# Scaling the three widest tiles of P on ScalarE in batches 0 and 1 of a decay attention with two feed-forward layers

## Chip, cores and metric

The kernel runs on one core of a Trainium2 chip. The metric is the device time of one launch in microseconds (us); lower is better. Three runs of the kernel before took 909.36 to 911.1 us, with a median of 910.57.

## What is computed

Four batches of eight heads of causal attention with a decay that is added to the scores, over 576 positions of 64 values; its output, 2304 rows of 512, goes through a feed-forward layer with Mish (2048 wide) and then through one with a maximum of three products (768 wide).

```python
def _attn_ref(q, k, v, f):
    scores = scale * np.matmul(q, k.transpose(0, 1, 3, 2))
    cum = np.cumsum(np.log(np.clip(f, 0.0001, 1.0)), axis=-1)
    decay = cum[:, :, :, None] - cum[:, :, None, :]
    scores = np.where(causal, -1000000000.0, scores + decay)
    attn = np.exp(scores - np.max(scores, axis=-1, keepdims=True))
    attn = attn / (np.sum(attn, axis=-1, keepdims=True) + 1e-09)
    return np.matmul(attn, v)
def _moe_ref(x, w_in, w_out):
    h = x @ w_in
    return (h * np.tanh(softplus(h))) @ w_out
def _moe2_ref(x, w1, w2, w3, w_out):
    return np.maximum(np.maximum(x @ w1, x @ w2), x @ w3) @ w_out
```

## The kernel before

**Attention.** Two heads make a pair; a batch has four pairs, so there are 16 pairs, eight of them in batches 0 and 1. A pair is done in two units of `scores`. Unit g = 0 makes four tiles of P: for each head 128 query rows against 128 keys, and 128 against 256. Unit g = 1 makes five: for each head 128 rows against 384 keys and against 512, and one tile with the last 64 rows of both heads against all 576 (its name is `P_None`). The index of a tile within its unit is `ci`, so that in unit 1 the tiles 2, 3 and 4 are the two of 512 columns and the one of 576.

Each tile passes through these steps. TensorE makes the scores (`sc`, L336). VectorE adds the decay `cb` and finds the row's extreme `mn` (L390). ScalarE takes the exponential in place and sums each row into `sums` (L396). When a part of the unit's tiles is through, the helper `scale_rows` lets VectorE add 1e-9 to the sums (L357) and take the reciprocals `rr` (L358), and GpSimd multiplies each tile by its column of `rr` (L360). Unit 0 has two such parts, of tiles 0, 1 and 2, 3; in unit 1 they are tiles 0, 1 and tiles 2 to 4. TensorE then turns the scaled P in blocks of 128 x 128 (`pp`, L429), VectorE and ScalarE by turns copy the result out of PSUM (`TA` and `TB`, L433 and L435), and TensorE multiplies by v (`av`, L415). ScalarE rounds the result to a high part `xh` (L131) and VectorE keeps the rest as `xl` (L137).

Before a pair's scores, q and k are turned on TensorE (`tr`, L312) and copied by ScalarE as `kT` and `qT` (L314, L315, L317). Three PSUM banks are shared by these turned tiles and by `pp`. GpSimd masks the decay tiles `cb` (L295, L299), which come by DMA.

**Conversion of w_in.** Beside the attention the first layer's weights, which lie in 64-bit numbers, are fetched (`wr`, L146, 16 transfers) and converted: ScalarE takes the absolute value (Abs, L156), GpSimd clamps it (L160), VectorE shifts and joins the bits in three steps (L163, L166, L170), ScalarE rounds to the high part `wi` (L131) and GpSimd subtracts for the low part (L137).

**The first layer** (`h`, L181 to L183, three products each of high and low parts) is run by TensorE between the steps of the attention, as soon as the rows of a block and a piece of w_in are there. After the last `h`, the rest is nearly TensorE's alone: `y`, `g`, `q` and `o`.

**Order.** Every engine runs its instructions in the order in which they were put on its queue. That order isn't the order of the program text: a list scheduler with a model of times sets it, by priorities. `scale_rows` has a raised priority.

Of the kernel before, what the change touches and what calls it, by code (L numbers as in the profile page):

```python
# [13 lines left out]
AF = mybir.ActivationFunctionType  # L14
# [18 lines left out]
BLK = 256  # L33
BLK2 = 512
LEAD = 2

# [26 lines left out]
def tile_decay_attention__mish_ff__max3_ff(  # L65
# [16 lines left out]
    nc = tc.nc  # L82
# [8 lines left out]
    scale = 1.0 / float(D) ** 0.5  # L91
# [186 lines left out]
    def decay(J, h, qt):  # L278

        c2, c4 = J["cb"]  # L280
        if h is None:
            return c4.rearrange("p (a c) -> p a c", c=288)
        t = c2[:, h]
        if qt == 0:
            return t[:, 5:6, :]
        if qt == 1:
            return t[:, 0:7:6, :]
        if qt == 2:
            return t[:, 0:3, :].rearrange("p b c -> p (b c)")[:, None, :]
        return t[:, 0:6, :].rearrange("p (a b) c -> p a (b c)", a=2)[:, :, 0:256]  # L290
# [10 lines left out]
    def prep(J):  # L301

        b, hp, raw = J["b"], J["hp"], J["raw"]
        qq = as_.tile([128, 512], F32, name="qT", bufs=2)
        kk = as_.tile([128, S], F32, name="kT", bufs=2)
        last, v_ = q4[J["i"] % 2], vs[J["i"] % 3]
        rest = att_psum("tr")
        for i, dst in ((1, kk), (0, qq)):
            tr = att_psum("tr")
            with queued(last_av):  # L310
                for c in range(4):
                    nc.tensor.transpose(tr[:, c * 128:c * 128 + 128], raw[i][:, c * 128:c * 128 + 128], ident)  # L312
                last_tr[:] = [nc.tensor.transpose(rest[:, i * 64:i * 64 + 64], raw[i][U, 512:640], ident[U, U])]
            nc.scalar.activation(dst[:, 0:512], tr, AF.Copy)  # L314
        nc.scalar.activation(kk[:, 512:S], rest[:, 64:128], AF.Copy)  # L315
        for h, rows in enumerate((U, L)):
            nc.scalar.activation(last[rows, h * 64:h * 64 + 64], rest[rows, 0:64], AF.Copy)  # L317
        for h in range(2):
            nc.sync.dma_start(
                v_[:, h * 256:(h + 1) * 256].rearrange("p (t d) -> p t d", t=4),  # L320
                v[b, 2 * hp + h, 0:512, :].rearrange("(t p) d -> p t d", t=4),
            )
        nc.sync.dma_start(
            v_[L, 512:640].rearrange("p (h d) -> p h d", h=2),
            v[b, 2 * hp:2 * hp + 2, 512:S, :].rearrange("h p d -> p h d"),
        )
        J.update(q=qq, q4=last, k=kk, vs=v_)
        mask_decay(J)

    def score_mm(J, h, qt, dst, c0, w):  # L330
        if h is None:
            lhs, rows = J["q4"], slice(0, 128)
        else:
            rows = (U, L)[h]
            lhs = J["q"][rows, qt * 128:qt * 128 + 128]
        nc.tensor.matmul(dst, lhs, J["k"][rows, c0:c0 + w], start=True, stop=True, skip_group_check=True)  # L336

    def scores(J, g):


        P = {}
        u = count["unit"]
        count["unit"] += 1
        sm = sums[u % 4]
        mn = aw.tile([128, 6], F32, name="mn", bufs=4)
        rr = aw.tile([128, 5], F32, name="rr", bufs=4)
        tiles = [(h, qt) for qt in ((0, 1) if g == 0 else (2, 3)) for h in range(2)]
        if g == 1:
            tiles.append((None, 4))
        made = []  # L350
        col = 0

        def scale_rows(part):

            cs = slice(part[0], part[-1] + 1)
            with tc.high_priority(400):
                nc.vector.tensor_scalar(rr[:, cs], sm[:, cs], 1e-9, None, op0=ALU.add)  # L357
                nc.vector.reciprocal(rr[:, cs], rr[:, cs])  # L358
                for ci in part:
                    nc.gpsimd.tensor_scalar(made[ci], made[ci], rr[:, ci:ci + 1], 1.0, op0=ALU.mult, op1=ALU.mult)  # L360

        for ci, (h, qt) in enumerate(tiles):
            wd = (qt + 1) * 128 if qt < 4 else S
            Pt = aw.tile([128, wd], F32, name=f"P{qt}_{h}", bufs=LEAD)
            made.append(Pt)
            if h is None:
                P[4] = Pt
            else:
                P[h, qt] = Pt
            cb = decay(J, h, qt)  # L370
            if h is None:
                cb = [cb[:, n:n + 1] for n in range(2)]
            else:
                cb = [cb]
            s0 = 128 if qt == 1 else 0
            if not h and qt != 1:
                count["sc"] += 1
                pair = (aps if count["sc"] % 2 or not eps else eps[0]).tile([128, 2, 512], F32, name="sc", bufs=1)
                for n in range(2):
                    if h is None:  # L380
                        score_mm(J, h, qt, pair[:, n, :288], 288 * n, 288)
                    else:
                        score_mm(J, n, qt, pair[:, n, :wd], 0, wd)
                if qt == 0:
                    for n in range(2):
                        score_mm(J, n, 1, pair[:, n, 128:384], 0, 256)
            for pi, (c0, w) in enumerate([(0, wd)] if qt < 4 else [(0, 288), (288, 288)]):
                sc = pair[:, h or pi, s0:s0 + w]
                like = lambda t: t.rearrange("p (a c) -> p a c", a=cb[pi].shape[1])
                nc.vector.tensor_tensor_reduce(  # L390
                    out=like(Pt[:, c0:c0 + w]), in0=like(sc), in1=cb[pi],
                    scale=-scale, scalar=(3e38 if pi == 0 else mn[:, col - 1:col]),
                    op0=ALU.add, op1=ALU.min, accum_out=mn[:, col:col + 1],
                )
                col += 1
            nc.scalar.activation(  # L396
                Pt, Pt, AF.Exp, scale=-1.0, bias=mn[:, col - 1:col], accum_out=sm[:, ci:ci + 1],
            )
            if ci == 1:
                scale_rows([0, 1])  # L400
        scale_rows(list(range(2, len(tiles))))
        return P

# [48 lines left out]
    def attention():  # L452
# [9 lines left out]
        pend = []  # L462
        for n in range(len(units) + LEAD):
            if n == 6 + LEAD:
                eps.clear()
                early.close()
                eps_h.append(sa.enter_context(tc.tile_pool(name="hps", bufs=2, space=PSUM, reuse_waits="tile")))
            if n < len(units):
                ji, g = units[n]
                pend.append((J[ji], g, scores(J[ji], g)))  # L470
            if n >= LEAD:
                unit = pend.pop(0)
# [5 lines left out]
            if n < len(units) and g == (ji == 0) and ji + 1 < len(jobs):  # L478
                prep(J[ji + 1])
            if n >= LEAD:  # L480
                next(rest, None)
# [315 lines left out]
    for ft in range(NF2):  # L797
        g = [gps[ft % 2].tile([128, BLK2], F32, name=f"g{m}") for m in range(3)]
# [126 lines left out]
```

## Time and profile before

| | |
|---|---|
| median of 3 runs | 910.57 us (909.36 to 911.1) |
| the profiled execution | 909.78 us |
| its span, first to last instruction | 907.7 us |
| mean granted clock of TensorE | 0.992 of full speed |
| busy: TensorE, VectorE, ScalarE, GpSimd | 97%, 55%, 44%, 26% of the span |

The rows are read as follows. A group of instructions shows its line, engine, operation, output and inputs, shapes and count, then the busy time in us, the mean of one in ns, and the idle time just before with what ended it. A wait reads "engine line waited for engine line: us in total, times, the longest". PE is TensorE, PEld its weight loads, DVE VectorE, ACT ScalarE, POOL GpSimd, SP the queue that issues most DMAs.

### The profile page before, as it was taken

How to read it: one execution, taken by the hardware profiler on the slowest of the kernel's cores; microseconds unless marked ns; L12 is line 12 of the kernel's file. 1: busy time of each engine (PE TensorE's matmuls, PEld its weight loads, DVE VectorE, ACT ScalarE, POOL GpSimd, SP SyncE). 2: the span in 40 equal slices, each digit the busy share in tenths (PEclk: the TensorE clock that was granted, in tenths of full speed). 3: DMA queues.
4: the chain of work that ended last, by engine and by line, in shares of the span. 5: the costliest groups of instructions: out<-in, count | busy, mean ns of one | idle time of the engine just before them, and what ended most of it. 6: DMA issues, size and time to landing. Idle time of an engine off the chain costs nothing.

```text
span 907.7 us, 13930 instructions
## 1 busy us (share of the span) xinstructions
PE 882.8 (97%) x4800; PEld 704.8 (78%) x4800; DVE 497.1 (55%) x1186; ACT 400.7 (44%) x913; POOL 232.7 (26%) x317
## 2 busy tenths in 40 slices
PE   6898999999999999999999999999999999999998
PEld 3565666767767778889888888889888998889986
DVE  3598675344444343991367575775855447424440
ACT  4687666454443432533465545553433222412211
POOL 3689987222222220000020000000121332013310
PEclk8989999999999999999999999999999999999999
DMA  7896664444333115863456666663499444333401
GB/s 183 227 226 171 179 192 117 115 134 127 105 102 108 47 48 178 292 226 128 143 181 217 214 216 222 217 226 98 162 359 322 124 123 117 111 96 126 139 23 60
DMA packets 125030, 145.25 MB, mean 160 GB/s; under 512 B 64736, under 2 KB 78048, under 8 KB 124960
## 3 DMA queue, kind: packets, MB, share of 16 engines
q1 hardware_dynamic: 105856, 102.41, 39.0%
q10 hardware_dynamic: 16416, 27.79, 8.3%
q0 software_dynamic: 2688, 14.16, 4.3%
q8 instruction: 38, 0.62, 0.3%
q14 instruction: 32, 0.26, 0.1%
HBM read 102.83 MB, written 41.49 MB: 159 GB/s over the span
## 4 chain that ended last, share of the span: by engine, by line
PE 89%; POOL 3%; DMA 2%; DVE 2%; issue 1%; ACT 1%; SPq 1%; POOLq 0%
PE y L181 7%; PE y L183 7%; PE y L182 7%; PE h L181 7%; PE h L182 7%; PE h L183 7%; PE q L182 6%; PE q L183 6%; PE q L181 6%; PE sc L336 5%; PE av L415 5%; PE pp L429 5%; PE o L181 3%; PE o L182 3%; PE o L183 3%; PE g L181 2%
## 5 line engine op out<-in xcount | busy, mean ns | idle before, releaser
L181 PE MATMUL h<-xh,wi 128*128 128x512 f32 (+1 forms) x320 | 121.4, 380 | 1.6 <-ACT he L522 1.3
L182 PE MATMUL h<-xl,wi 128*128 128x512 f32 (+1 forms) x320 | 120.6, 377 | 1.8 <-DVE xl L137 1.8
L183 PE MATMUL h<-xh,wi 128*128 128x512 f32 (+1 forms) x320 | 120.7, 377 | 0.0
L182 PE MATMUL y<-gl,wo 128*128 128x512 f32 (+1 forms) x320 | 117.7, 368 | 0.0
L183 PE MATMUL y<-gh,wo 128*128 128x512 f32 (+1 forms) x320 | 117.6, 368 | 0.0
L181 PE MATMUL y<-gh,wo 128*128 128x512 f32 (+1 forms) x320 | 106.3, 368 | 0.0
L360 POOL TENSOR_SCALAR P<-P,rr 128x128 f32<-128x128 f32 (+3 forms) x128 | 74.0, 592 | 87.5 <-DVE rr L358 31.5
L659 DVE TENSOR_TENSOR gl<-g,gh 128x512 fp32r<-128x512 f32 x72 | 50.0, 697 | 83.3 <-ACT gh L658 83.1
L396 ACT ACTIVATE P<-P,mn 128x128 f32<-128x128 f32 (+3 forms) x128 | 70.7, 554 | 53.4 <-DVE mn L390 50.2
L652 ACT ACTIVATE g<-g 128x512 f32<-128x512 f32 x72 | 45.2, 632 | 70.6 <-DMA g<-h_d 65.7
L181 PEld LDWEIGHTS h<-xh,wi 128*128 128x128 f32 x320 | 60.1, 188 | 14.6 <-issue 2.2
L182 PEld LDWEIGHTS h<-xl,wi 128*128 128x128 f32 x320 | 60.1, 188 | 14.0 <-issue 2.8
L183 PEld LDWEIGHTS h<-xh,wi 128*128 128x128 f32 x320 | 60.3, 188 | 11.5 <-issue 2.7
L182 PEld LDWEIGHTS y<-gl,wo 128*128 128x128 f32 x320 | 60.3, 188 | 10.2
L183 PEld LDWEIGHTS y<-gh,wo 128*128 128x128 f32 x320 | 60.2, 188 | 10.1
L181 PEld LDWEIGHTS y<-gh,wo 128*128 128x128 f32 x320 | 60.3, 189 | 10.1
L522 ACT ACTIVATE he<-h 128x512 f32<-128x512 f32 x56 | 33.3, 595 | 57.0 <-PE h L183 52.4
L851 DVE TENSOR_TENSOR u<-q,p 128x448 f32<-128x448 f32 x36 | 22.4, 621 | 62.3 <-PE q L183 60.7
L336 PE MATMUL sc<-kT,qT 64*128 64x128 f32 (+3 forms) x256 | 51.9, 500 | 3.6 <-DVE mn L390 3.3
L429 PE MATMUL pp<-ident,P 128*128 128x128 f32 x320 | 51.1, 285 | 4.0 <-ACT qT L314 3.6
L658 ACT ACTIVATE gh<-g 128x512 fp32r<-128x512 f32 x72 | 45.0, 627 | 22.0 <-PE y L183 20.9
L429 PEld LDWEIGHTS pp<-ident,P 128*128 128x128 f32 x320 | 37.0, 143 | 20.1 <-issue 5.0
(141 smaller groups left out, 1850.3 us busy)
## 6 DMA issues: line engine op xcount, KB each, us to landing
g<-h_d SPq DMA_DIRECT2D x72, 256.0 KB, 2.9
s<-s_d SPq DMA_DIRECT2D x72, 256.0 KB, 3.0
h_d<-he ACTq DMA_DIRECT2D x56, 256.0 KB, 2.9
wr<-in_moe_w_out_dram SPq DMA_DIRECT2D x22, 512.0 KB, 4.6
wr<-in_moe_w_dram SPq DMA_DIRECT2D x24, 384.0 KB, 3.8
s_d<-sk POOLq DMA_DIRECT2D x12, 768.0 KB, 5.8
cb<-cum_d SPq DMA_DIRECT2D x32, 256.0 KB, 4.2
wr<-in_moe_w_in_dram SPq DMA_DIRECT2D x16, 512.0 KB, 4.5
```

What stands on the lines that cost most here:

```text
L181: nc.tensor.matmul(ps, wh, xh, start=start, stop=False, skip_group_check=True)
L182: nc.tensor.matmul(ps, wh, xl, start=False, stop=False, skip_group_check=True)
L183: return nc.tensor.matmul(ps, wl, xh, start=False, stop=stop, skip_group_check=True)
L336: nc.tensor.matmul(dst, lhs, J["k"][rows, c0:c0 + w], start=True, stop=True, skip_group_check=True)
L360: nc.gpsimd.tensor_scalar(made[ci], made[ci], rr[:, ci:ci + 1], 1.0, op0=ALU.mult, op1=ALU.mult)
L396: nc.scalar.activation(Pt, Pt, AF.Exp, scale=-1.0, bias=mn[:, col - 1:col], accum_out=sm[:, ci:ci + 1],)
L415: last = nc.tensor.matmul(acc[(U, L)[h], off:off + w], J["vs"][:, n * 64:n * 64 + 64], T[:, at[h]:at[h] + w], start=kt == 0 and off == 0, ...
L429: turn = nc.tensor.transpose(pp[:, n * 128:n * 128 + 128], Pt[:, k0:k0 + 128], ident)
L522: nc.scalar.activation(he, h, AF.Copy)
L652: nc.scalar.activation(g, g, AF.Mish)
L658: on_act[:] = [nc.scalar.activation(gh, g, AF.Copy)]
L659: on_dve[:] = [nc.vector.tensor_tensor(out=gl, in0=g, in1=gh, op=ALU.subtract)]
```

## The change

A table names, by unit, the tiles that ScalarE scales in batches 0 and 1. The others in these batches and all tiles of batches 2 and 3 stay with GpSimd. ScalarE's operation is a Copy with the reciprocals as a scale for each row.

```diff
+ON_ACT = {0: (), 1: (2, 3, 4)}
...
                 for ci in part:
+                    if J["b"] < 2 and ci in ON_ACT[g]:
+                        nc.scalar.activation(made[ci], made[ci], AF.Copy, scale=rr[:, ci:ci + 1])
+                        continue
                     nc.gpsimd.tensor_scalar(made[ci], made[ci], rr[:, ci:ci + 1], 1.0, op0=ALU.mult, op1=ALU.mult)
```

Since the scheduler sets the order anew, it differs on every engine from about the second pair until the first layer's end. In the changed kernel the lines up to L359 stand one further down and those from L360 on four (L156 is now L157, L360 is L364); the new operation is L362.

ScalarE around the first conversion, before (Abs is L156; the tiles 724, 730 and 737 belong to the third pair):

```order
L314 ACTIVATE kT<-tr 128x512
L396 ACTIVATE P_0_724,sums_172<-P_0_724,mn 128x384
L156 ACTIVATE wt<-wr 128x512
L396 ACTIVATE P_1_730,sums_172<-P_1_730,mn 128x384
L156 ACTIVATE wt<-wr 128x512
L314 ACTIVATE qT<-tr 128x512
L315 ACTIVATE kT<-tr 128x64
L317 ACTIVATE q_1_189<-tr 64x64 x2
L131 ACTIVATE xh_446<-av 128x256
L396 ACTIVATE P_0_737,sums_172<-P_0_737,mn 128x512
```

The same place now (Abs is L157; 518, 524 and the first P_None are the second pair's tiles):

```order
L362 ACTIVATE P_0_518<-P_0_518,rr 128x512
L362 ACTIVATE P_1_524<-P_1_524,rr 128x512
L362 ACTIVATE P_None<-P_None,rr 128x576
L400 ACTIVATE P_0_724,sums_172<-P_0_724,mn 128x384
L400 ACTIVATE P_1_730,sums_172<-P_1_730,mn 128x384
L157 ACTIVATE wt<-wr 128x512 x2
L315 ACTIVATE kT<-tr 128x512
L400 ACTIVATE P_0_737,sums_172<-P_0_737,mn 128x512
L316 ACTIVATE kT<-tr 128x64
L318 ACTIVATE q_1_189<-tr 64x64 x2
L400 ACTIVATE P_1_743,sums_172<-P_1_743,mn 128x512
L315 ACTIVATE qT<-tr 128x512
```

The second pair's three scalings stand ahead of the two Abs, as the first pair's do some rows further up. kT has moved from ahead of the Abs to behind both, and qT behind two exponentials of 512 columns.

GpSimd in the third pair, before:

```order
L160 TENSOR_SCALAR wt<-wt 128x512 x2
L360 TENSOR_SCALAR P_0_724<-P_0_724,rr 128x384
L360 TENSOR_SCALAR P_1_730<-P_1_730,rr 128x384
L137 TENSOR_TENSOR wi_148<-wt,wi_148 128x512
L295 AFFINE_SELECT cb<-cb 128x2x256
L295 AFFINE_SELECT cb<-cb 128x2x128 x2
L360 TENSOR_SCALAR P_0_737<-P_0_737,rr 128x512
L360 TENSOR_SCALAR P_1_743<-P_1_743,rr 128x512
L360 TENSOR_SCALAR P_None<-P_None,rr 128x576
L160 TENSOR_SCALAR wt<-wt 128x512
L299 TENSOR_TENSOR cb_819<-cb_819,mask_110 128x64
L360 TENSOR_SCALAR P_0_844<-P_0_844,rr 128x128
```

And now:

```order
L161 TENSOR_SCALAR wt<-wt 128x512
L364 TENSOR_SCALAR P_0_724<-P_0_724,rr 128x384
L364 TENSOR_SCALAR P_1_730<-P_1_730,rr 128x384
L161 TENSOR_SCALAR wt<-wt 128x512
L296 AFFINE_SELECT cb<-cb 128x2x256
L138 TENSOR_TENSOR wi_148<-wt,wi_148 128x512
L296 AFFINE_SELECT cb<-cb 128x2x128 x2
L300 TENSOR_TENSOR cb_819<-cb_819,mask_110 128x64
L364 TENSOR_SCALAR P_0_844<-P_0_844,rr 128x128
```

The three wide scalings are gone, and the next pair's first tile (844) follows the masks of cb at once.

## Rows read from the trace of the kernel before

**Rows 1.** The page's first part: busy time, share of the span, instructions.

```profile
PE 882.8 (97%) x4800; PEld 704.8 (78%) x4800; DVE 497.1 (55%) x1186; ACT 400.7 (44%) x913; POOL 232.7 (26%) x317
```

**Rows 2.** Stretches: length; PE, PEld, DVE, ACT, POOL busy (count); clock; DMA share, GB/s.

```profile
0.00:20.00 20.00, 11.36 (x38) 6.80 (x40) 6.41 (x29) 8.37 (x24) 4.99 (x20) 0.86 0.77 183
20.00:45.00 25.00, 21.36 (x143) 12.20 (x139) 15.19 (x66) 16.59 (x50) 16.75 (x32) 0.98 0.83 220
...
45.00:50.00 5.00, 4.62 (x22) 3.64 (x23) 4.63 (x14) 4.40 (x15) 3.52 (x4) 0.51 1.05 234
...
45.00:147.00 102.00, 94.22 (x631) 65.00 (x632) 82.02 (x225) 70.97 (x198) 94.50 (x99) 0.97 0.67 178
...
160.00:880.00 720.00, 719.60 (x3801) 593.34 (x3800) 387.69 (x845) 293.64 (x616) 110.84 (x156) 1.00 0.49 158
```

**Rows 3.** Waits of VectorE from 45 to 147 us.

```profile
DVE wt L163 <- POOL wt L160: 15.0, 10, 3.2
```

**Rows 4.** Groups of GpSimd's instructions from 45 to 147 us, forms kept apart.

```profile
L160 POOL TENSOR_SCALAR wt<-wt 128x512 f32<-128x512 f32 x16 | 30.8, 1927 | 3.7 <-ACT wt L156 2.9
...
L360 POOL TENSOR_SCALAR P<-P,rr 128x512 f32<-128x512 f32 x10 | 9.0, 907 | 0.3
...
L360 POOL TENSOR_SCALAR P_None<-P_None,rr 128x576 f32<-128x576 f32 x5 | 4.1, 829 | 0.0
```

**Rows 5.** Timeline of TensorE: start, length, operation, idle before and what ended it.

```profile
79.79 0.50 PE L182 MATMUL h<-xl,wi 128*128 128x512 f32 x1 [1.80 <-DVE xl L137]
...
85.13 0.92 PE L336 MATMUL sc<-kT,qT 64*128 64x384 f32 x4 [1.25 <-DVE mn L390]
...
106.83 0.88 PE L336 MATMUL sc<-kT,qT 64*128 64x384 f32 x2 [2.00 <-DVE mn L390]
...
145.97 0.50 PE L181 MATMUL h<-xh,wi 128*128 128x512 f32 x1 [1.32 <-ACT he L522]
```

**Rows 6.** The chain of work that ended last: start, length in us, what.

```profile
79.27 1.93 POOL wt L160
...
93.30 5.30 DMA cb<-cum_d
...
138.27 1.93 POOL wt L160
```

**Rows 7.** Groups of ScalarE's instructions, 45 to 147 us, and the last over the span.

```profile
L131 ACT ACTIVATE wi<-wt 128x512 fp32r<-128x512 f32 x16 | 10.0, 628 | 14.5 <-DVE wt L170 14.5
...
L396 ACT ACTIVATE P<-P,mn 128x512 f32<-128x512 f32 x12 | 8.6, 714 | 0.0
...
L396 ACT ACTIVATE P_None<-P_None,mn 128x576 f32<-128x576 f32 x16 | 12.4, 772 | 11.4 <-DVE mn L390 11.3
```

**Rows 8.** Busy time in the stretch from 25 to 35 us.

```profile
25.00:35.00 10.00, 9.89 (x67) 5.73 (x63) 8.66 (x41) 8.80 (x30) 8.04 (x16) 1.00 0.74 180
```

**Rows 9.** Timeline of SyncE's queue, ScalarE and TensorE: start, length, operation, idle before.

```profile
37.07 2.42 SPq L146 DMA_DIRECT2D wr<-in_moe_w_in_dram  x4
...
42.48 0.66 ACT L156 ACTIVATE wt<-wr 128x512 f32<-128x512 f32 x1 [3.85 <-DMA wr<-in_moe_w_in_dram]
...
44.75 0.58 ACT L314 ACTIVATE qT<-tr 128x512 f32<-128x512 f32 x1
...
45.38 1.11 PE L429 MATMUL pp<-ident,P 128*128 128x128 f32 x4 [3.61 <-ACT qT L314]
46.42 1.65 PE L336 MATMUL sc<-kT,qT 64*128 64x128 f32 x8
```

**Rows 10.** Timeline of GpSimd and of VectorE near 77 us.

```profile
77.21 1.26 POOL L137 TENSOR_TENSOR wi<-wt,wi 128x512 fp32r<-128x512 f32 x1
...
77.31 1.71 DVE L170 SCALAR_TENSOR_TENSOR wt<-wr,wt 128x512 int32<-128x512 int32 x1
```

**Rows 11.** One group of VectorE from 45 to 147 us, and from 160 to 350.

```profile
L357 DVE TENSOR_SCALAR rr<-sums 128x2 f32<-128x2 f32 x15 | 6.8, 450 | 0.5 <-ACT P L396 0.4
...
L357 DVE TENSOR_SCALAR rr<-sums 128x2 f32<-128x2 f32 x22 | 3.6, 166 | 7.9 <-ACT P L396 7.8
```

## The prediction

> **What bounds the kernel now.** The page's first part comes first: TensorE is busy 882.8 of 907.7 us [rows 1], so a change off TensorE can give back only its idle time, some 25 us. The table by stretches says where that lies [rows 2]: 8.6 us before 20 us, 3.6 from 20 to 45, 7.8 from 45 to 147, 0.4 from 160 to 880; what is left of the 25, some 4.5, lies nearly all after 880. The matmuls are the same before and after; a TensorE that never waits again after 147 us only begins earlier or later. So what the change is worth is settled before 147 us, and comes out at the end one for one.
>
> From 45 to 147 us GpSimd is busy 94.5 of 102 us, VectorE 82.0, ScalarE 71.0 [rows 2]. That is the stage in which w_in is converted beside attention. The waits agree: VectorE waits 15.0 us for GpSimd's clamp (L160), ten times, and ScalarE 14.5 us for the last step of the same conversion (L170) [rows 3, 7]. What GpSimd does there is 30.8 us of clamps, the low halves of w_in (L137), and scaling of P; the widest three tiles of five pairs are 9.0 + 4.1 = 13.1 us of it [rows 4].
>
> TensorE's timeline puts names to its idle time [rows 5]: 1.80 us before 80 us for xl, 1.25 before 85 and 2.00 before 107 for VectorE's score reduction, 1.32 before 146 for the copy of h. The chain of waits leads to the gap at 85 us from a clamp that began at 79.27, to the one at 146 from a clamp of 138.27, and to the one at 107 from a cb transfer of 5.30 us that began at 93.30 [rows 6].
>
> **What goes away on GpSimd.** Sixteen scalings of 512 columns and eight of 576, all of batches 0 and 1. Five pairs of them lie between 45 and 147 us and cost 13.1 us there [rows 4]; the other three lie where GpSimd isn't full. After the change GpSimd has 94.5 - 13.1 = 81.4 us in this stage, VectorE still 82.0, ScalarE 71.0 + 10 = 81. No engine is clearly last then: VectorE is late next, with TensorE itself at 94.2 of 102. In the new order the 24 operations are gone from GpSimd's queue, and the next pair's work and the clamps move up behind the 384-column scalings.
>
> How much of the 13.1 us TensorE gets is bounded by its idle time. None at all is the lower end: VectorE's order could take up everything. All 7.8 us of idle is the upper. I count three gaps that hang on GpSimd: 1.80, 1.25 and 1.32, together **4.4 us**. The 2.00 us gap I leave out, because its chain runs through that cb transfer, which the change doesn't shorten. Until 78 us GpSimd has been spared two pairs, 2/5 of 13.1 = 5.2 us, more than the 1.80 + 1.25 of the two gaps up to there, so the relief is large enough for them; whether the order lets it through is the open point.
>
> **What is added on ScalarE.** No row shows a plain scaled copy of P. The nearest is a copy of 512 columns from SBUF to SBUF, 628 ns; the upper bound is the exponential of the same tile, 714 ns, and 772 ns at 576 columns [rows 7]. With the copy's price and 58 ns more for 64 columns (772 - 714) a pair costs 2 x 0.63 + 0.69 = 1.95 us, with the exponential's 2 x 0.71 + 0.77 = 2.2. I take **2.0**, the copy being the same kind of work without a sum kept: 16 us over eight pairs, 10 us in the five of the full stage. Copy already stands between the exponentials (the evacuations of L435), so it needs no table of its own. The Trainium skill, page "ScalarE: Activation LUTs", section "Rules for kernel authors", speaks against the move: it gives multiplications to VectorE rather than ScalarE, and budgets about 0.3 us per ACTIVATE plus 0.83 ns per element. By that, an estimate, a pair would cost 2.23 us; the trace's 628 ns at 512 columns is under its 725.
>
> From 45 to 147 us ScalarE has 31 us idle, and 14.5 of it is that wait for VectorE, so I cost the 10 us there at nothing. If that cover is gone, what waits behind a triple (the three wide scalings of a pair) is the next exponentials and the copies that free the transpose banks.
>
> **The ramp has no such cover.** Between 25 and 35 us ScalarE is busy 8.8 of 10 us, while TensorE is busy 9.9 and GpSimd 8.0 [rows 8]. The new order puts two triples there, 2 x 1.95 = 3.9 us, ahead of the first w_in conversion. Before, ScalarE reached the first Abs (L156) at 38.6 us and stood 3.85 us until the transfer landed, with qT behind it; TensorE stood 3.61 us for qT [rows 9]. The w_in transfers are issued from 37.07 on a queue that waits little, so they should land as before, at 42.5 and 44.2. The triples fill ScalarE's idle 3.85 us; that is their cover. But now both Abs, kT, two exponentials of 512 columns and the small copies stand ahead of qT. Before, qT followed the second Abs at 44.75 [rows 9]. Now kT begins there, and between it and qT stand two exponentials at 0.71 [rows 7] with their sums and some small copies: I put qT's begin near 47.5 and its end near 48.1, where it ended at 45.3. The next pair's scores, which began at 46.42 and need qT, begin near 48.1: **1.7 us lost**. The bounds are 0 (the transpose banks are free earlier by kT, and work fills in) and 2.8 (the whole delay of qT). TensorE's granted clock from 45 to 50 us was 0.51, its lower level of 1.2 GHz, after the 3.61 us stop [rows 2, 9]. The stop stays in some form, so I count no change.
>
> **Sum.** -4.4 + 1.7 = -2.7 us. The profiled execution took 909.78 us (span 907.7 and 2.1 around it), which gives 907.1; the median of the runs is 0.79 above it, so 910.57 - 2.7 = **907.9 us**.
>
> **Rivals.**
> *GpSimd's relief is taken up by VectorE (no change).* For it: VectorE runs in order, 82.0 of 102 us, and a step of the conversion itself, an L170 of 1.71 us, stands ahead of the xl for which TensorE waited 1.80 us; GpSimd's low half ran beside it, and that stays [rows 10]. Against: GpSimd is the fuller by 12 us. Half of 4.4 would be left: -2.2 + 1.7 = -0.5, **910.1 us**. That the change doesn't reach its aim at all is excluded: the new order shows the 24 operations on ScalarE's queue.
>
> *ScalarE's queue holds up TensorE (slower).* The mechanism is the triple itself: it waits for the pair's reciprocals, and the kT and qT copies, exponentials and evacuations behind it wait too. Place: the two in the ramp and the five up to 147 us. Each triple that falls on TensorE's path in full costs 2.0 us; against 4.4 gained it decides from 2.2 triples on, and with three and a half the result is +2.6, **913.2 us**. For it: ScalarE at 8.8 of 10 in the ramp. Against: its 31 us idle in the full stage, and that in the new order one to five other operations stand between a pair's last exponential and its triple.
>
> *The whole stage comes free (faster still).* VectorE's small operations are stretched where GpSimd is full: L357 on two columns takes 450 ns from 45 to 147 us and 166 after 160 [rows 11]. That is 15 x 0.284 = 4.3 us of VectorE's 82 on this form alone. If less GpSimd work gives VectorE this back too, all 7.8 us of idle from 45 to 147 us go; with half the ramp's loss, 0.8, that is -7.0, **903.6 us**. The Trainium skill, "SBUF — State Buffer", section "Who interferes with whom", has the rule behind this: GpSimd and VectorE share a port pair as an exclusive lock, while ScalarE never waits on anyone. By that rule each of the 24 operations moved takes a blocker away from VectorE, and the time would be that of this rival; the trace agrees as far as the stretched L357, though the clamps and the low halves stay on GpSimd.
>
> **How the numbers follow.** The forecast has 0.48, no change 0.20, slower 0.18, the whole stage free 0.14. A measurement here tells about 0.2%, 1.8 us, from no change. Faster by more than that: 0.42 of the forecast's 0.48 and all of 0.14, 0.56. Slower: most of its rival and a little of the no-change case, 0.18. The rest, 0.26, is within. The range runs from 904.0, near the free stage, to 912.5, short of the slower rival: the part of both beyond it is under 0.2.
>
> **What would show it.** Right: GpSimd near 81 us where 147 us stood before as the end of the conversion, and that end some microseconds earlier; VectorE's wait for L160 well under 15 us; the scaling on ScalarE near 0.63 and 0.69 us; qT near 48 us and TensorE's stop there still over 3 us in sum; TensorE's idle time from 45 to 147 us down from 7.8 to about 3.4. Wrong: idle time of TensorE unchanged with GpSimd's down (the first rival), waits of TensorE for kT, qT, TA or TB behind ScalarE's scaling (the second), or any new idle time after 160 us.

## The result, and the profile after

The changed kernel takes 921.13 us (median of 4 runs, 920.17 to 921.6) where the kernel before takes 910.08 beside it. The ratio is 1.0119, with a 95% interval from 1.0103 to 1.0135: 11 us slower. The forecast was 907.9 us in a range from 904.0 to 912.5, so both the side and the range are missed.

The page's first part of the changed kernel, whose span is 919.8 us, answers to [rows 1]:

```profile
PE 891.0 (97%) x4800; PEld 709.1 (77%) x4800; DVE 496.1 (54%) x1186; ACT 416.2 (45%) x937; POOL 212.3 (23%) x293
```

GpSimd has 20 us less work, ScalarE 15 more, as intended. TensorE does the same matmuls, but is busy 8.2 us longer, and its idle time (span less busy) is 28.8 us where it was 24.9. Those are the 12.1 us of span. Of the added busy time 4.9 us lie in the scores of P, first before, then now:

```profile
L336 PE MATMUL sc<-kT,qT 64*128 64x128 f32 (+3 forms) x256 | 51.9, 500 | 3.6 <-DVE mn L390 3.3
```

```profile
L337 PE MATMUL sc<-kT,qT 64*128 64x128 f32 (+3 forms) x256 | 56.8, 510 | 3.2 <-DVE mn L394 2.4
```

In the mean one of the 256 is 10 ns longer, 2.6 us for all; the rest is that they overlap less.

The table by stretches of the changed kernel (columns as in [rows 2]) shows where:

```profile
40.00:60.00 20.00, 15.57 (x64) 8.73 (x62) 12.90 (x43) 16.22 (x44) 14.95 (x18) 0.66 0.84 228
45.00:147.00 102.00, 92.99 (x585) 61.42 (x584) 72.88 (x200) 72.83 (x185) 75.80 (x76) 0.91 0.62 168
160.00:880.00 720.00, 718.37 (x3824) 591.53 (x3823) 384.96 (x852) 298.17 (x630) 111.46 (x161) 1.00 0.50 160
```

and one row of the kernel before that did not stand ahead of the prediction:

```profile
40.00:60.00 20.00, 16.39 (x107) 10.96 (x103) 15.05 (x51) 16.09 (x47) 16.34 (x21) 0.83 0.91 250
```

From 45 to 147 us GpSimd came down from 94.5 [rows 2] to 75.8 us, and VectorE from 82.0 to 72.9. No engine but TensorE is near full any more. Still TensorE is idle 9.0 of these 102 us, where it was 7.8, and its granted clock is 0.91 where it was 0.97. From 40 to 60 us the clock is 0.66 (0.83 before), and 64 matmuls begin where 107 did. After 160 us little is new: 1.2 us more of idle time.

The groups of the changed kernel from 45 to 147 us, forms kept apart, answer to [rows 3, 4, 11]:

```profile
L161 POOL TENSOR_SCALAR wt<-wt 128x512 f32<-128x512 f32 x15 | 30.1, 2006 | 5.1 <-ACT wt L157 4.3
...
L164 DVE TENSOR_SCALAR wt<-wt 128x512 int32<-128x512 int32 x15 | 14.3, 950 | 13.1 <-POOL wt L161 13.1
...
L362 ACT ACTIVATE P<-P,rr 128x512 f32<-128x512 f32 x10 | 6.6, 708 | 0.0
...
L362 ACT ACTIVATE P_None<-P_None,rr 128x576 f32<-128x576 f32 x5 | 3.8, 761 | 0.0
...
L358 DVE TENSOR_SCALAR rr<-sums 128x2 f32<-128x2 f32 x12 | 2.4, 200 | 1.6 <-ACT P L400 1.6
```

and one group of the kernel before:

```profile
L163 DVE TENSOR_SCALAR wt<-wt 128x512 int32<-128x512 int32 x16 | 9.6, 601 | 15.0 <-POOL wt L160 15.0
```

VectorE still waits 13.1 us for the clamps (15.0 before). Its first step of the conversion, L164 (L163 before), takes 950 ns where it took 601; the small L358 takes 200 ns where it took 450 [rows 11].

### The profile page after: what moved, and what is told of

Same layout as the page of the kernel before. It is cut to its first block, busy times and chain, and to the rows that moved or that the text cites. A ratio compares the mean times of both kernels' runs of the same rounds, so it can differ in the third digit from the quotient of the medians.

```text
span 919.8 us, 13927 instructions
## 1 busy us (share of the span) xinstructions
PE 891.0 (97%) x4800; PEld 709.1 (77%) x4800; DVE 496.1 (54%) x1186; ACT 416.2 (45%) x937; POOL 212.3 (23%) x293
## 4 chain that ended last, share of the span: by engine, by line
PE 85%; DVE 3%; DMA 3%; POOL 3%; ACT 2%; issue 2%; SPq 1%; POOLq 0%; DVEq 0%; ACTq 0%
PE y L182 7%; PE y L184 7%; PE y L183 7%; PE h L182 6%; PE h L184 6%; PE h L183 6%; PE q L183 6%; PE q L182 6%; PE q L184 6%; PE sc L337 5%; PE av L419 5%; PE pp L433 4%; PE o L182 3%; PE o L183 3%; PE o L184 3%
## 5 line engine op out<-in xcount | busy, mean ns | idle before, releaser
L364 POOL TENSOR_SCALAR P<-P,rr 128x128 f32<-128x128 f32 (+3 forms) x112 | 60.5, 554 | 112.5 <-DVE rr L359 62.5
L184 PEld LDWEIGHTS h<-xh,wi 128*128 128x128 f32 x320 | 60.3, 188 | 10.8 <-issue 1.5
L184 PEld LDWEIGHTS y<-gh,wo 128*128 128x128 f32 x320 | 60.3, 189 | 10.1
L182 PEld LDWEIGHTS y<-gh,wo 128*128 128x128 f32 x320 | 60.3, 189 | 10.1
L183 PEld LDWEIGHTS h<-xl,wi 128*128 128x128 f32 x320 | 60.2, 188 | 10.1 <-issue 1.3
L337 PE MATMUL sc<-kT,qT 64*128 64x128 f32 (+3 forms) x256 | 56.8, 510 | 3.2 <-DVE mn L394 2.4
L433 PEld LDWEIGHTS pp<-ident,P 128*128 128x128 f32 x320 | 36.5, 144 | 23.6 <-issue 10.1
```

The costliest lines, as they stand in the source:

```text
L182: nc.tensor.matmul(ps, wh, xh, start=start, stop=False, skip_group_check=True)
L183: nc.tensor.matmul(ps, wh, xl, start=False, stop=False, skip_group_check=True)
L184: return nc.tensor.matmul(ps, wl, xh, start=False, stop=stop, skip_group_check=True)
L433: turn = nc.tensor.transpose(pp[:, n * 128:n * 128 + 128], Pt[:, k0:k0 + 128], ident)
```

## The experiments

Times are compared by the ratio to the kernel before in the same series of runs; one thousandth is 0.9 us.

### Operations and order apart

The change does two things: it moves 24 operations, and it makes the scheduler plan everything anew. The instructions carry the same numbers in both kernels, so an order can be taken from one and imposed on the other. `ORDER` holds each engine's instructions in the order of the kernel before, the 24 left out, and `pin` chains them; a link says only which of two instructions of an engine stands first and adds no wait. The 24 go where the scheduler puts them. Edit to the changed kernel:

```diff
+ORDER = """
...
+def pin(tc):
+    traced = {i.name: i for i in tc.nc.cur_bb.bb.instructions}
+    for names in planned():
+        for first, then in zip(names, names[1:]):
+            tc.add_manual_dep(
+                traced[then], first,
+                mybir.DependencyInfo(mybir.DependencyClass.NoSync, mybir.DependencyReason.DATA),
+                reason="pin",
+            )
...
         tile_decay_attention__mish_ff__max3_ff(tc, *args)
+        pin(tc)
```

> The changed kernel, with every other instruction held to the order that it has in the kernel before, on all five engines; only ScalarE's 24 scalings are placed by the scheduler. Order theory (the 11 us come from the order that the scheduler made anew, which puts the conversion of w_in ahead of attention): 906 to 911 us, TensorE at half clock for some 7 us before 160 us as in the kernel before. Queue theory (ScalarE's scalings themselves hold up kT, qT, TA and TB): 916 to 922 us, waits of TensorE for ScalarE of some microseconds more than before.

Measured: 906.02 us, ratio 0.9961 (0.9946 to 0.9976). The 24 operations, in the order of before, gain 3.5 us. The page's first part (span 903.6 us):

```profile
PE 881.1 (98%) x4800; PEld 703.9 (78%) x4800; DVE 492.9 (55%) x1186; ACT 414.7 (46%) x937; POOL 212.2 (23%) x293
```

the same stretches:

```profile
40.00:60.00 20.00, 15.71 (x114) 10.28 (x114) 15.55 (x55) 17.60 (x50) 15.71 (x20) 1.00 1.03 270
45.00:147.00 102.00, 96.32 (x652) 66.13 (x653) 79.30 (x231) 81.60 (x215) 80.09 (x85) 0.98 0.69 184
```

and groups from 45 to 147 us:

```profile
L164 DVE TENSOR_SCALAR wt<-wt 128x512 int32<-128x512 int32 x15 | 8.7, 580 | 9.7 <-POOL wt L161 9.7
...
L358 DVE TENSOR_SCALAR rr<-sums 128x2 f32<-128x2 f32 x15 | 5.0, 332 | 2.4 <-ACT P L400 2.4
```

TensorE's idle time is 22.5 us over the span, 5.7 from 45 to 147 us; VectorE's wait for the clamp fell to 9.7 us. The clock is full from 40 to 60 us.

The second experiment is the cross: the kernel before, with all but the 24 operations pinned to the order of the changed kernel.

```diff
-ORDER of the kernel before, under the changed kernel
+ORDER of the changed kernel, under the kernel before (the 24 scalings on GpSimd)
```

> The kernel before, GpSimd scaling everything, with every other instruction held to the order that it has in the changed kernel. Order theory: 919 us or more, as slow as the changed kernel or slower, since GpSimd has 13 us more to do in the same order; the half-clock stretches near 42 to 56 us and after 76 us are there. Queue theory: 909 to 912 us, since nothing is added to ScalarE.

Measured: 925.4 us, ratio 1.0168 (1.0153 to 1.0183). Page and group (span 923.5 us):

```profile
PE 892.7 (97%) x4800; PEld 709.1 (77%) x4800; DVE 496.0 (54%) x1186; ACT 401.3 (43%) x913; POOL 229.7 (25%) x317
```

```profile
L163 DVE TENSOR_SCALAR wt<-wt 128x512 int32<-128x512 int32 x16 | 15.1, 944 | 17.3 <-POOL wt L160 17.3
```

So the new order costs 15.3 us with the scalings on GpSimd (1.0168) and 14.4 with them on ScalarE (1.0119 against 0.9961), while the move gains 3.5 us in the old order and 4.5 in the new. Operations and order add up, and ScalarE's scalings hold up nobody in sum: the queue theory falls. No run pins a kernel to its own order. But if the links themselves cost or gave time, each pinned kernel would have it, and two further pinned kernels below, each with a part of the scalings, gain 2.1 and 1.6 us, together about the 3.5 of this one.

### Parts of the change, planned freely

```diff
-                    if J["b"] < 2 and ci in ON_ACT[g]:
+                    if J["b"] == 0 and ci in ON_ACT[g]:
```

> Only the four pairs of batch 0 go to ScalarE, the scheduler plans anew. Order theory: the time follows what the new plan does between 40 and 60 us; if that stretch looks as in the changed kernel (TensorE's clock at 0.66 from 40 to 60 us), 914 to 921 us. Queue theory: half of the triples, half of the loss, about 915 to 916 us.

```diff
-                    if J["b"] < 2 and ci in ON_ACT[g]:
+                    if J["b"] == 1 and ci in ON_ACT[g]:
```

> Only the four pairs of batch 1 go to ScalarE, the scheduler plans anew; the ramp keeps its operations. Order theory: the clock near 0.83 from 40 to 60 us as in the kernel before, and 905 to 913 us, by what the plan does from 80 us on. Queue theory: half of the triples, half of the loss, about 915 to 916 us.

Measured: 918.92 us (1.0096, 1.0079 to 1.0112) and 917.68 us (1.0088, 1.0066 to 1.0109). Each half costs 8 to 9 us, not half of 11: a second sign that it isn't the number of triples that counts. With batch 1 alone the ramp is untouched, the clock from 40 to 60 us is full, and the loss comes all the same. The order theory's 905 to 913 us for it was wrong: a new plan behind the ramp costs too.

### Which stretch, which queue

Two orders were joined at the fourth pair's last exponential (near 60 us): everything that one kernel's plan has up to there, then the rest as the other has it. In two more kernels single queues were exchanged. All have the scalings on ScalarE.

```diff
-ORDER of the kernel before
+ORDER of the changed kernel up to that exponential, the order of before for the rest
```

> The operations of the changed kernel; the new order up to the fourth pair's last exponential (it ends at 60.9 us in the changed kernel), the order of the kernel before from there. Ramp theory (the loss is made by the longer half-clock stretch from 42 to 56 us and what follows from it): 918 to 921 us. Spread theory (every stage of the new order loses something; until 60 us some 4 us against the old order): 909 to 912 us, with the lower clock near 42 to 56 us.

```diff
-ORDER of the kernel before
+ORDER of before up to that exponential, the order of the changed kernel for the rest
```

> The operations of the changed kernel; the order of the kernel before up to the fourth pair's last exponential, the new order from there. Ramp theory: 905 to 908 us. Spread theory: 914 to 918 us, with TensorE's gaps between 70 and 100 us and the half-clock stretches behind them still there.

Measured: 913.28 us (1.0032, 1.002 to 1.0045) and 920.55 us (1.0121, 1.0096 to 1.0146). Against the first experiment the new order costs 6.5 us in the ramp and 14.6 after it. The sum is above the 14.4 of both together, so the parts are not independent; but the ramp alone is not the cause.

```diff
-ORDER of the kernel before
+ORDER of the changed kernel for TensorE, VectorE, ScalarE, GpSimd; of before for SyncE
```

> The operations and the new order of the changed kernel on TensorE, VectorE, ScalarE and GpSimd; SyncE's queue, which issues the loads, held to its order of before. If the re-ordered loads (cb, raw q and k, v behind w_in) are what makes attention late: 906 to 912 us. If the order of the computing engines is: 918 to 922 us.

```diff
-ORDER of the kernel before
+ORDER of the changed kernel for GpSimd; of before for the other four
```

> The operations of the changed kernel in the order of before, but GpSimd in its new order, which puts clamps and low halves of w_in ahead of the small scalings of P. If this order of GpSimd is the cause: 915 us or more. If the cause lies in the order of VectorE, ScalarE and TensorE: 905 to 909 us.

Measured: 930.84 us (1.0221, 1.02 to 1.0242) and 916.97 us (1.0079, 1.0064 to 1.0094). The new order of the loads isn't what hurts: the old one beside the new plan makes it worse still. GpSimd's new queue alone, with every other queue as before, costs 10.7 us. Such a mixture has a cost of its own, though: GpSimd's clamps, now early, stand there 16.9 us for ScalarE's Abs, which is still late, against 3.5 us in the first experiment and 4.3 in the changed kernel (from 45 to 147 us). So the two runs show that the queues depend on each other, not what each queue costs in the changed kernel.

### The ramp by itself

```diff
-                    if J["b"] < 2 and ci in ON_ACT[g]:
+                    if 2 <= J["i"] < 8 and ci in ON_ACT[g]:
```

The order of the kernel before is pinned here and in the next.

> The order of the kernel before on all engines; only the pairs 2 to 7 (18 scalings) go to ScalarE, the two pairs of the ramp stay with GpSimd. By the prediction's terms (relief 4.4 us, no cost in the ramp): 905 to 906 us. If the moves in the ramp were part of the gain of the first experiment: 907.5 us or more.

```diff
-                    if J["b"] < 2 and ci in ON_ACT[g]:
+                    if J["i"] < 2 and ci in ON_ACT[g]:
```

> The order of the kernel before on all engines; only the pairs 0 and 1 (6 scalings, in the ramp) go to ScalarE. By the prediction's term for the ramp (+1.7 us): 911 to 912 us. If the ramp costs nothing in this order: 908 to 910 us.

Measured: 907.59 us (0.9977, 0.9964 to 0.999) and 908.75 us (0.9982, 0.9971 to 0.9993). In the old order the pairs 2 to 7 gain 2.1 us and the two of the ramp 1.6. Together that is about the first experiment's 3.5. The intervals are wide: 0.9 to 3.3 us and 0.6 to 2.6.

### Early conversion, or the order of the attention

The two orders differ most visibly in the conversion of w_in. Counted in the order, the first VectorE step of a transfer of w_in stands, on average over the 16, behind 138 VectorE instructions of other work in the kernel before and behind 127 in the changed one. Two crosses part this from the order of the attention. In the first the 128 instructions that fetch and convert w_in are left out of `ORDER` (of before), and the scheduler puts them early.

```diff
-ORDER of the kernel before
+ORDER of the kernel before, without the 128 instructions of the conversion
```

> The operations of the changed kernel; the attention and all else in the order of before, only the 128 instructions that load and convert w_in are placed by the scheduler, which puts them as early as in the changed kernel (the seventh block's first VectorE step stands behind 120 of its other instructions, 135 in the kernel before and 117 in the changed one). If the early conversion is what costs: 914 us or more. If it is the order of the attention itself: 904 to 909 us.

Measured: 914.26 us, ratio 1.0039 (1.0027 to 1.0052), 7.1 us over the first experiment. Page (span 913.1 us) and group:

```profile
PE 884.1 (97%) x4800; PEld 706.0 (77%) x4800; DVE 493.2 (54%) x1186; ACT 415.2 (45%) x937; POOL 214.7 (24%) x293
```

```profile
L164 DVE TENSOR_SCALAR wt<-wt 128x512 int32<-128x512 int32 x16 | 9.8, 614 | 16.4 <-POOL wt L161 16.2
```

TensorE's busy time is 3.0 us above the first experiment's and its idle time 29.0 us, 6.5 above. VectorE's wait for the clamp is 16.2 us. The place can be read. VectorE in this kernel:

```profile
63.89 0.42 DVE L138 TENSOR_TENSOR xl<-av,xh 128x256 fp32r<-128x256 f32 x1 [0.63 <-ACT xh L132]
68.41 1.48 DVE L164 TENSOR_SCALAR wt<-wt 128x512 int32<-128x512 int32 x1 [4.10 <-POOL wt L161]
69.93 0.69 DVE L167 SCALAR_TENSOR_TENSOR wt<-wr,wt 128x512 int32<-128x512 int32 x1
70.65 0.98 DVE L171 SCALAR_TENSOR_TENSOR wt<-wr,wt 128x512 int32<-128x512 int32 x1
71.56 0.21 DVE L138 TENSOR_TENSOR xl<-av,xh 128x64 fp32r<-128x64 f32 x1
```

GpSimd:

```profile
66.06 0.31 POOL L300 TENSOR_TENSOR cb<-cb,mask 128x64 f32<-128x64 f32 x1 [1.81 <-DMA cb<-cum_d]
66.46 1.92 POOL L161 TENSOR_SCALAR wt<-wt 128x512 f32<-128x512 f32 x1
```

ScalarE, whose xh the small xl needs:

```profile
66.11 0.23 ACT L132 ACTIVATE xh<-av 128x64 fp32r<-128x64 f32 x1
```

TensorE:

```profile
71.82 1.54 PE L419 MATMUL av<-TA,vs 128*64 128x256 f32 x8 [4.42 <-DVE xl L138]
```

and VectorE at the same place of the first experiment:

```profile
60.41 0.42 DVE L138 TENSOR_TENSOR xl<-av,xh 128x256 fp32r<-128x256 f32 x1
63.97 0.23 DVE L138 TENSOR_TENSOR xl<-av,xh 128x64 fp32r<-128x64 f32 x1 [3.13 <-ACT xh L132]
```

VectorE comes to L164 at 64.3 us, because the plan puts this conversion step ahead of the small xl. Its clamp has not begun: it stands on GpSimd behind the last masking of cb, which waits 1.81 us for its transfer. VectorE stands 4.10 us, then does the three steps, and xl comes at 71.56, although xh has been there since 66.34; the first experiment has xl at 63.97. TensorE waits 4.42 us for it. The conversion of one transfer ahead of one small subtraction costs TensorE more than the 3.5 us that the 24 operations gain.

The other cross keeps the new order of the attention and puts GpSimd's conversion steps behind the same attention steps as in the kernel before; the conversion steps of the other engines are placed by the scheduler and follow these.

```diff
-ORDER of the kernel before
+ORDER of the changed kernel without the conversion; GpSimd's conversion at its old places
```

> The operations of the changed kernel and its new order for the attention; GpSimd's conversion steps stand behind the same attention steps as in the kernel before, and those of the other engines follow (the seventh block's first VectorE step behind 133). If the early conversion is what costs: 905 to 912 us. If the order of the attention itself does: 917 us or more.

Measured: 915.46 us, ratio 1.0053 (1.0033 to 1.0072), 6.0 us under the changed kernel and 8.4 over the first experiment. The profiled execution is the shortest of its four, 3.2 us under their median (span 910.5 us):

```profile
PE 887.2 (97%) x4800; PEld 708.9 (78%) x4800; DVE 492.3 (54%) x1186; ACT 416.4 (46%) x937; POOL 211.3 (23%) x293
```

```profile
L164 DVE TENSOR_SCALAR wt<-wt 128x512 int32<-128x512 int32 x15 | 8.7, 579 | 9.0 <-POOL wt L161 9.0
```

```profile
40.00:60.00 20.00, 15.40 (x62) 8.63 (x60) 12.33 (x40) 15.46 (x42) 14.82 (x18) 0.66 0.81 225
```

The wait for the clamp is 9.0 us and the idle time 23.3, nearly the first experiment's. What is left is busy time, 887.2 us against 881.1, with the clock from 40 to 60 us at 0.66 and 62 matmuls there. So by these two crosses the loss has two parts of like size, 7.1 and 8.4 us of 14.4: early conversion, which stops TensorE, and the new order of the attention, in which TensorE takes longer over the same matmuls. The early places in the first cross are the scheduler's for that kernel and not those of the changed one, and some 3 us of the second part stand in no profile.

### One unlucky plan?

Two small edits make the scheduler plan anew for other reasons, each without the move and with it:

```diff
-                for ci in part:
+                for ci in reversed(part):
```

> Nothing is moved to ScalarE; within each part the tiles are scaled in reversed order, widest first, which makes the scheduler plan anew (conversion a little earlier: on average its VectorE steps stand behind 134 other instructions, 138 in the kernel before). If any new plan costs: 917 us or more. If the cost comes from the plan that a relieved GpSimd gives: 909 to 914 us.

> The changed kernel with the same reversal of the tiles within a part: a third plan for the moved scalings, with the conversion as early as in the changed kernel (on average behind 128; 127 in the changed kernel). If the loss is the early conversion and what it does to the attention's order: 915 to 922 us. If the changed kernel's plan was one unlucky draw: 904 to 912 us.

```diff
-RATE = 2.0
+RATE = 1.9
```

> The kernel before with RATE 1.9, another reason for a new plan (it differs from about the seventh pair on; conversion on average behind 139). If any new plan costs: 915 us or more. If the cost comes from the plan that a relieved GpSimd gives: 907 to 913 us.

> The changed kernel with RATE 1.9 (conversion on average behind 128). If the loss is systematic for plans with the scalings on ScalarE: 915 to 923 us. If it was one unlucky draw: 904 to 912 us.

| kernel | scalings on ScalarE | first conversion step behind | time | ratio and interval |
|---|---|---|---|---|
| before | none | 138 | 909.41 | 1 |
| reversed | none | 134 | 915.01 | 1.0067 (1.0052 to 1.0082) |
| RATE 1.9 | none | 139 | 913.19 | 1.005 (1.0033 to 1.0067) |
| changed | 24 | 127 | 921.13 | 1.0119 (1.0103 to 1.0135) |
| changed, reversed | 24 | 128 | 916.4 | 1.0079 (1.0064 to 1.0094) |
| changed, RATE 1.9 | 24 | 128 | 918.93 | 1.0109 (1.0094 to 1.0124) |

Both readings are half right. Every new plan here costs: two that move nothing lose 4.5 and 6.1 us, so the plan of the kernel before is a good one among its like. And the plans for the moved scalings are the worse ones: three lose 7.2 to 10.8 us, although their operations are worth some 4 us. All three have the conversion early. That the scheduler's model finds GpSimd free and fills it is my reading; no run shows it. Early conversion can't be all of it: the two half moves are new plans as well, and counted in their traces, batch 0 alone has the first conversion step behind 128 instructions and loses 8.7 us, but batch 1 alone has it behind 135, near the 138 of before, and loses 8.0. Five plans against two are few, and the two edits may cost something besides their plans (`RATE` sets how many steps of the first layer are woven in beside a step of the attention). The size of this second part is not settled.

The unmoved plan with RATE 1.9 shows that the clock isn't needed for a loss. Its stretches:

```profile
40.00:60.00 20.00, 15.26 (x113) 9.94 (x112) 15.44 (x52) 16.24 (x49) 17.35 (x21) 1.00 0.97 263
45.00:147.00 102.00, 88.88 (x624) 60.86 (x623) 82.11 (x223) 69.12 (x192) 93.70 (x98) 1.00 0.66 180
```

The clock is full throughout, and TensorE is idle 13.1 of 102 us.

### The stop in the ramp

The first experiment with one edit in ScalarE's part of `ORDER`, written here by what its instructions are:

```diff
 L315 kT
 L400 P 128x384
-L157 Abs
 L400 P 128x384
-L157 Abs
 L315 qT
 L316 kT
 L318 q x2
+L157 Abs x2
 L132 xh
```

> The first experiment (scalings moved, order of before) with one edit of ScalarE's order: the first two Abs of the conversion stand behind qT, the last part of kT and the second 384-column exponential, not ahead of them. If TensorE's stop near 42 us is ScalarE standing in order for the w_in transfer: the stop falls from 2.6 us to under 1 us, no lower clock behind it, 903 to 905 us. If the conversion, begun later, gives it back by 147 us: 906 us as in the first experiment.

Measured: 906.67 us, ratio 0.9962 (0.9949 to 0.9976): neither better nor worse than the first experiment. ScalarE and TensorE there:

```profile
40.35 0.58 ACT L315 ACTIVATE qT<-tr 128x512 f32<-128x512 f32 x1
...
43.01 0.67 ACT L157 ACTIVATE wt<-wr 128x512 f32<-128x512 f32 x1 [0.91 <-DMA wr<-in_moe_w_in_dram]
...
45.39 0.58 ACT L439 ACTIVATE TB<-pp 128x512 f32<-128x512 f32 x1
```

```profile
46.02 0.69 PE L433 MATMUL pp<-ident,P 128*128 128x128 f32 x2 [2.46 <-ACT TB L439]
```

qT now ends at 40.93 us, but the second Abs still stands 0.91 us for its transfer, and the copy of TB, behind it and two exponentials of 512 columns, comes at 45.39. TensorE stops 2.46 us for that copy. The stop has moved to the next copy in ScalarE's queue; the clock behind it fell again (0.66 from 45 to 50 us).

## Why the prediction was wrong

**What bounds the kernel: right in the place, wrong in the kind.** The time was settled before 147 us, but for the 1.2 us of idle time after 160, and GpSimd was the fullest engine but TensorE. Relief of GpSimd alone, in an unchanged order, does shorten the kernel: 0.9961. But the prediction counted only idle time as at stake, since the matmuls are the same. 8.2 of the 12.1 us of span came as busy time, for which the sum had no place.

**The relief, -4.4 us: mis-sized by half.** In the old order the pairs 2 to 7 gain 2.1 us. TensorE's idle time from 45 to 147 us falls from 7.8 to 5.7, not to 3.4. GpSimd came to 80.1 us there, near the 81.4 that was worked out.

**The ramp, +1.7 us: wrong in sign in the old order.** The two pairs of the ramp gain 1.6 us. In the new order the delay of qT has the form predicted, only milder. ScalarE in the changed kernel:

```profile
36.50 1.33 ACT L362 ACTIVATE P<-P,rr 128x512 f32<-128x512 f32 x2
37.73 0.78 ACT L362 ACTIVATE P_None<-P_None,rr 128x576 f32<-128x576 f32 x1
...
40.97 0.66 ACT L157 ACTIVATE wt<-wr 128x512 f32<-128x512 f32 x1 [1.28 <-DMA wr<-in_moe_w_in_dram]
43.02 0.67 ACT L157 ACTIVATE wt<-wr 128x512 f32<-128x512 f32 x1 [1.38 <-DMA wr<-in_moe_w_in_dram]
43.59 0.57 ACT L315 ACTIVATE kT<-tr 128x512 f32<-128x512 f32 x1
...
46.17 0.60 ACT L315 ACTIVATE qT<-tr 128x512 f32<-128x512 f32 x1
```

and TensorE:

```profile
44.31 2.17 PE L433 MATMUL pp<-ident,P 128*128 128x128 f32 x8 [3.85 <-ACT kT L315]
46.83 1.65 PE L337 MATMUL sc<-kT,qT 64*128 64x128 f32 x8 [0.35 <-ACT qT L315]
```

qT ends at 46.8 us, 1.4 behind the kernel before, not 2.8; the scores begin 0.4 us later, not 1.7. A triple takes 2.0 us (36.50 to 38.51), as priced, though one scaling alone takes 708 or 761 ns, more than the 630 and 690 forecast. It fills ScalarE's wait for the transfer, of which 1.28 us are left. The w_in transfers did not land as before: they were issued from 36.02 us, not 37.07, and the first Abs began at 40.97, not 42.48. Yet the ramp as a whole is dearer than the term: the new order up to 60 us costs 6.5 us in the join above, and the 0.4 us of the scores explain little of that.

With both terms the sum gives 907.9 us and the first experiment 906.0. As a forecast for the operations that is close by luck: -4.4 and +1.7 were forecast, -2.1 and -1.6 measured, and the errors cancel.

**The step that failed** is a term that the sum doesn't have. The prediction read from the new order that "the next pair's work and the clamps move up behind the 384-column scalings" and took that for part of the relief. It went through the new order in the ramp and priced nothing of it elsewhere. The order is worth four times the operations: +14.4 us. Two sentences of the prediction point at it without a price: that VectorE runs in order, with conversion steps ahead of what TensorE waits for, and that "whether the order lets it through is the open point". The trace of the kernel before held a third sign: its chain to the gap at 107 us goes on from the cb transfer through a clamp at 101.01 and the three conversion steps of VectorE, 102.95 to 105.57 us, which stand ahead of the reductions that TensorE waited 2.00 us for.

How it hurts in the changed kernel is the pattern of the eleventh experiment, in smaller pieces. Its VectorE:

```profile
90.20 0.63 DVE L164 TENSOR_SCALAR wt<-wt 128x512 int32<-128x512 int32 x1 [1.10 <-POOL wt L161]
90.86 0.79 DVE L167 SCALAR_TENSOR_TENSOR wt<-wr,wt 128x512 int32<-128x512 int32 x1
91.57 0.28 DVE L394 CUSTOM_DVE_ANT_0 P<-sc,cb 128x128 f32<-128x128 f32 x1
...
92.33 0.41 DVE L394 CUSTOM_DVE_ANT_1 P<-sc,cb 128x256 f32<-128x256 f32 x1
```

GpSimd:

```profile
87.71 2.46 POOL L161 TENSOR_SCALAR wt<-wt 128x512 f32<-128x512 f32 x1
```

and TensorE, with its waits for a copy of TA and for these score reductions, and the scores that they reduce:

```profile
75.38 0.66 PE L313 MATMUL tr<-ident,rawq 128*128 128x128 f32 x4 [1.86 <-DVE TA L437]
...
88.53 0.93 PE L337 MATMUL sc<-kT,qT 64*128 64x128 f32 x8
...
92.90 1.00 PE L337 MATMUL sc<-kT,qT 64*128 64x384 f32 x4 [2.38 <-DVE mn L394]
```

A clamp that stands early on GpSimd's queue ends at 90.17 us. VectorE waits for it 1.10 us, does two conversion steps, and only then the reductions of four tiles, whose scores TensorE made at 88.53 to 89.46. TensorE waits 2.38 us. Moving the clamps up is therefore no relief for VectorE while its own conversion steps move up with them: it waited 15.0 us for clamps before, 13.1 in the changed kernel, 9.7 with the same operations in the old order.

**"The stop stays in some form, so I count no change" of the clock: wrong.** TensorE's stop is 3.85 us in the changed kernel and 3.61 before, but from 40 to 60 us the granted clock is 0.66 against 0.83, and 64 matmuls against 107. The clock's share in the loss is small all the same. The mean granted clock is 0.992 over 907.7 us before and 0.989 over 919.8 now: 7.3 and 10.1 us short of full speed, so by that (an estimate) some 3 of the 8.2 us of busy time at most. And of 60 executions of the kernel before, five have that mean of 0.989; they take 909.72 to 910.52 us. The rest of the 8.2 us is, as I read it, the sparser feed in the new order of the attention, to which the scores that overlap less point; no run tests that by itself.

**The rivals.** The slower one named the right side and the wrong mechanism. TensorE does wait for kT, TA and TB in the changed kernel, but ScalarE reaches kT late because it stands for the w_in transfer (1.28 and 1.38 us), not for the scalings; and where the scalings go back to GpSimd in the same order, the time rises by 4.5 us. VectorE taking up the relief comes nearest: it describes the path, and had it been priced by what may stand ahead of a score reduction, it might have ended on the slow side. The free stage saw its premise come true without its result: L358 fell from 450 to 200 ns. What VectorE gained there it lost in L164, 601 ns before and 950 now. Of the 15 from 45 to 147 us, eight begin when a subtraction of GpSimd (L138) has 0.7 us or more still to run, and take 1.03 to 1.50 us; the other seven take 0.41 to 0.63. In the kernel before one of 16 begins so, and in the first experiment one of 15. One of the eight, with its subtraction:

```profile
72.04 1.49 DVE L164 TENSOR_SCALAR wt<-wt 128x512 int32<-128x512 int32 x1 [0.23 <-POOL wt L161]
```

```profile
71.98 1.26 POOL L138 TENSOR_TENSOR wi<-wt,wi 128x512 fp32r<-128x512 f32 x1
```

It ends at 73.53 us, 0.29 after the subtraction, and the copy of TA for which TensorE waits 1.86 us stands behind it on VectorE. The Trainium skill, "SBUF — State Buffer", section "Who interferes with whom", says that of two instructions that want the shared port pair the later one is blocked whole; this row agrees.

## What to carry to other kernels

Where a scheduler sets the order, an edit is two edits: the operations and a new plan, and each wants its own experiment. Pinning all other instructions to the old order parts them in one run, and it gave the best kernel of this study, 0.4% faster than before, from a change that as planned costs 1.2%. Before an engine is relieved, read in the new order what background work moves up on the queues beside it, and price each step that now stands ahead of something TensorE waits for.

## What was not expected of the hardware

The ramp in the order of before gave stops of TensorE near 42 us of 3.61 us before, 2.60 in the first experiment and 2.10 with batch 1 alone; the first w_in transfer let ScalarE's Abs begin at 42.48, 41.37 and 41.93 us, and qT stands behind it. Behind the first the clock was 0.51 from 45 to 50 us, behind the other two 1.00; after the 2.46 us of the last experiment it was 0.66. A stop near this length can be followed by the lower clock or not, and over 60 executions of the kernel before the mean clock runs from 0.988 to 1.0, so one execution's clock there is no property of the kernel.
